# Windowed attention with a mixing layer: one f32 product for three f16 products in A times V

## The chip, the cores and the metric

The kernel runs on one core of a Trainium2 chip. The metric is device microseconds of one execution; of several runs the median is given.

## The reference

The input is q, k and v of 8 batches, 8 heads, 576 positions and 64 values each, in f32, and four weight matrices. Per head there is a causal attention with a window of 128 positions and a linear bias by distance; the heads' outputs, side by side, are x (576 x 512 per batch), which then goes through a mixing layer.

```python
scores = scale * np.matmul(q, k.transpose(0, 1, 3, 2))
mask = (rel >= 0) & (rel < window)
scores = np.where(mask, scores + bias[None], -1000000000.0)
scores = scores - np.max(scores, axis=-1, keepdims=True)
attn = np.exp(scores)
attn = attn / (np.sum(attn, axis=-1, keepdims=True) + 1e-09)
attn_out = np.matmul(attn, v)
# x: heads side by side
theta = x @ w_theta
zr, zi = x * np.cos(theta), x * np.sin(theta)
y = np.einsum('ts,bsd->btd', w_tok_r, zr) + np.einsum('ts,bsd->btd', w_tok_i, zi)
u = x + y
out = u + np.maximum(u @ w_ch, 0.0)
```

## The kernel before

Large products of f32 data are made from f16 parts: a matrix is scaled by a power of two and split into a high part (its f16 rounding) and a low part (the rest in f16), and three products of parts (high x high, high x low, low x high) take the place of one f32 product. q and k are split in the same manner into parts of an f32 format of the tensor engine.

**Heads, pairs, groups.** Heads are worked two at a time (class `Pair`, 32 pairs in all, 4 to a batch), and v is loaded for `GROUP = 4` heads at a time (16 groups, two to a batch; `load_values`, tile `vb`, 128 x 4 x 5 x 65 f32, in a pool `vbp`). The 65th column of v is one, so that the products of the weights with v give the denominator as well.

**One pair.** `Pair.scores` multiplies k and q, `weigh` adds the band and takes the row's extreme on VectorE (DVE, L417) and the exponential on ScalarE (ACT, L420). `Pair.flip` turns the unnormalised weights on the tensor engine (PE, L425), 4 tiles of 128 x 128 to a bank, and brings them to SBUF as `pt`. In batch 0 (`early`) that is one f32 copy on ACT (L428). In batches 1 to 7 ACT writes the high f16 part (L432) and DVE the low one (L433). `Head.values` multiplies `pt` with v (L461): 9 tile products to a head, each of which is three f16 products in batches 1 to 7 (27 to a head) and one f32 product in batch 0. `Head.finish` divides by the denominator (L467 to L470) and writes `x_sb`.

**v in f16.** For batches 1 to 7 `split_values` makes `vh` (ACT, L352, with a memset on GpSimd for the ones, L353) and `vl` (DVE, L354) once for each head. The scale of v comes from `measure` (a maximum of |v| for each head of the group, DVE, L252) and `spread_scales`: a transpose on PE (L259), a maximum, and a product with ones (L265) that brings the scales to all partitions (`spread`). It is called once for each group; for the second group of a batch `batch_scale` derives the factors that the mixing layer uses (`factors`).

**The mixing layer.** `turn` transposes x (L493), multiplies it with w_theta (L514), takes sine and cosine (L528 to L536) and makes z (L539), split into `z_hi` and `z_lo`. `mix` makes y from z and the token weights (L575), `channels` the last product (L597) and the output (L601 to L605).

**Order.** Batch 0's attention (`start`) runs beside the loading and splitting of the weight matrices (`unpack`). Then, per batch, `attend` runs the attention of the next batch in steps with `mix` and part of `channels` of this one; when all heads are done, `rotated` runs `turn` of the next batch beside the rest of `channels`. A planner turns this program order, with priority offsets (`MIX`, `CHAN`, `ROTATE`), into the order of each engine's queue; the offsets are constants in the source. DMAs are issued from SP's queue: q and k (`load_pair`), v (`load_values`), the output.

Of the kernel before, what the change touches and what calls it, by code (L numbers as in the profile page):

```python
# [11 lines left out]
F32 = mybir.dt.float32  # L12
# [3 lines left out]
F16 = mybir.dt.float16  # L16
# [10 lines left out]
PEXP = 14.0  # L27
# [11 lines left out]
RINGS = ([("mx", 2 * NT, 4)] + [("den", NT, 6)] + [("whole", 1, 3), ("vs", GROUP, 3), ("scale", GROUP, 4)]  # L39
         + [(name, width, 1) for name, width in (("whole0", 1), ("vs0", 11), ("scale0", 11), ("most0", 11), ("sum", 17),  # L40
# [11 lines left out]
def attn_moe_kernel(ctx: ExitStack, tc: tile.TileContext, qt, kt, vx, wth, wtok, wch, band, out):  # L52
# [6 lines left out]
    vp = ctx.enter_context(tc.tile_pool(name="vp", bufs=2))  # L59
    vbp = ctx.enter_context(tc.tile_pool(name="vbp", bufs=2))  # L60
# [170 lines left out]
    def load_plain(g):  # L231
        b, h = divmod(GROUP * g, H)
        vb = vbp.tile([128, GROUP, NT, 65], F32, name="vb")
        nc.sync.dma_start(out=vb, in_=vx[b, h:h + GROUP].rearrange("h p (c d) -> p h c d", d=65))
        return vb

# [52 lines left out]
    def measure_first(g):  # L289
        nc.vector.tensor_reduce(out=peaks[0][:, GROUP * g:GROUP * g + GROUP], in_=group_v[g][:, :, :, :64],  # L290
                                axis=mybir.AxisListType.XY, op=ALU.max, apply_absolute_value=True)

    FAMILIES = ((0, 1, 0, 2, 8, 2.0 ** 100), (5, 14, 2, 9, 9, 2.0 ** 120), (1, 5, 11, 4, 10, 2.0 ** 120))

    def scales_first():

        peak = peaks[0]
        for at, source in ((8, wide[:, :1]), (9, sums[:, 8:17]), (10, sums[:, 4:8])):
            nc.vector.tensor_reduce(out=peak[:, at:at + 1], in_=source, axis=mybir.AxisListType.X, op=ALU.max)
        nc.vector.tensor_scalar(out=peak[:, :8], in0=peak[:, :8], scalar1=2.0 ** -100, scalar2=None, op0=ALU.max)  # L300
        scale = spread(peak, 11, "0")
# [11 lines left out]
        nc.vector.tensor_tensor(out=scale[:, 10:11], in0=scale[:, 10:11], in1=rowt[:, 1:], op=ALU.mult)  # L313
        inverse(invs, rows)
        inverse(back, scale[:, 8:11])
# [9 lines left out]
        nc.vector.tensor_scalar(out=fac[:, 1:2], in0=scale[:, 8:9], scalar1=MAGIC, scalar2=None, op0=ALU.mult)  # L325
        batch_scale(0, scale[:, :8])
# [13 lines left out]

    def split_values(n):

        if n < H:
            if n % GROUP == 0:
                group_v[n // GROUP] = load_plain(n // GROUP)
            return (group_v[n // GROUP][:, n % GROUP],), None
# [5 lines left out]
        nc.scalar.activation(vh[:, :, :64], v, AF.Copy, scale=vs)  # L352
        nc.gpsimd.memset(vh[:, :, 64:], 1.0)  # L353
        nc.vector.scalar_tensor_tensor(out=vl, in0=v, scalar=vs, in1=vh[:, :, :64], op0=ALU.mult, op1=ALU.subtract)  # L354
        return (vh, vl), vs

# [11 lines left out]
    class Pair:  # L368


        def __init__(self, p):
            self.p = p
            self.terms = parts.pop(p)
            self.early = p < H // 2
# [47 lines left out]
        def flip(self, bank):  # L422
# [3 lines left out]
            if self.early:  # L426
                pt = ptp.tile([128, 512], F32, name="pt")
                nc.scalar.copy(pt, t_ps)  # L428
                parts_of = [pt]
            else:  # L430
                pt = ptp.tile([128, 2, 512], F16, name="pt")
                nc.scalar.activation(pt[:, 0], t_ps, AF.Copy, scale=2.0 ** PEXP)  # L432
                nc.vector.scalar_tensor_tensor(out=pt[:, 1], in0=t_ps, scalar=2.0 ** PEXP, in1=pt[:, 0],  # L433
                                               op0=ALU.mult, op1=ALU.subtract)
                parts_of = [pt[:, a] for a in range(2)]
            for n, (i, e, j) in enumerate(BANKS[bank]):
                for to in ((0, 1) if i == 0 else (e,)):
                    at = 128 * n + (64 * to if i == 0 else 0)
                    self.pt[i, to, j] = [t[:, at:at + 128] for t in parts_of]

    class Head:
        def __init__(self, n, pair):
            self.n, self.pair = n, pair
            self.b, self.h = divmod(n, H)
            self.tiny = 1.0e-9 * (1.0 if pair.early else 2.0 ** PEXP)

        def ready(self):
            self.v, self.vs = split_values(self.n)
# [383 lines left out]
```

## Time and profile before

| | |
|---|---|
| median of 3 runs | 777.27 us (776.39 to 779.42) |
| profiled execution | 778.7 us, span of its instructions 776.9 us |
| PE (matmul) busy | 695.1 us, 89% |
| PEld (weight load) busy | 520.1 us, 67% |
| DVE busy | 615.4 us, 79% |
| ACT busy | 500.9 us, 64% |
| POOL busy | 216.5 us, 28% |

Busy time is the union of an engine's instructions. Matmuls are pipelined and their ends are modelled, so the distance from one product's start to the next one's says more than a product's duration. Idle time of an engine is put down to the instruction that ended it (its releaser). `s_ps`, `t_ps`, `acc` and `mm` are banks of PSUM; `fixed` is a tile that holds many small operands.

### The profile page before, as it was taken

The page shows a single profiled execution, that of the slowest core. Times are in us where ns is not written, and L with a number is a line of the kernel's source. Part 1 is how long each engine was busy: PE and PEld are TensorE (multiplying, and loading weights), DVE is VectorE, ACT ScalarE, POOL GpSimd, SP SyncE. Part 2 cuts the span into 40 slices and gives each one's busy share as a digit, 9 for nine tenths or more (in the row PEclk, how much of TensorE's full clock was granted, in tenths as well). Part 3 has the DMA queues.
Part 4 walks back from the last instruction along what each step waited for, and adds up shares of the span by engine and source line. Part 5 has one row for each costly group of instructions (what it writes and reads, how often), then busy time and mean ns, then how long its engine had stood idle before and what let it go on. Part 6 is the DMA issues. An engine that isn't in the chain of part 4 may idle for free.

```text
span 776.9 us, 16320 instructions
## 1 busy us (share of the span) xinstructions
PE 695.1 (89%) x6236; PEld 520.1 (67%) x6239; DVE 615.4 (79%) x1668; ACT 500.9 (64%) x964; POOL 216.5 (28%) x237
## 2 busy tenths in 40 slices
PE   4698669789898999899989999899989998999997
PEld 2457555478756886578757885688657875787675
DVE  6998876977877986888688986798688877884844
ACT  4786526676478747786577747775678748754620
POOL 3523211400253113611171115311361116201700
PEclk9775558999999999999999999999999999999999
DMA  8353211121202220123003120132012300101001
GB/s 287 122 168 131 88 35 32 31 66 32 89 24 57 87 74 31 54 67 97 32 24 104 33 81 31 48 96 72 31 57 67 97 24 32 40 2 32 24 8 62
DMA packets 32623, 49.89 MB, mean 64 GB/s; under 512 B 5664, under 2 KB 22048, under 8 KB 32544
## 3 DMA queue, kind: packets, MB, share of 16 engines
q1 hardware_dynamic: 32544, 48.84, 20.3%
q8 instruction: 49, 0.80, 0.4%
q14 instruction: 30, 0.25, 0.1%
HBM read 39.39 MB, written 9.44 MB: 63 GB/s over the span
## 4 chain that ended last, share of the span: by engine, by line
PE 49%; DVE 26%; ACT 16%; issue 4%; DMA 4%; POOL 1%; SPq 0%; DVEq 0%; ACTq 0%; POOLq 0%
PE mm L575 20%; PE acc L461 6%; PE t_ps L425 6%; PE s_ps L402 6%; PE mm L597 5%; DVE f L529 4%; DVE g L531 3%; ACT g L535 3%; PE mm L514 3%; ACT s_sb L420 3%; DVE g L539 2%; ACT f L528 2%; DVE ql L335 2%; DVE x_lo L506 1%; DVE s_sb L417 1%
## 5 line engine op out<-in xcount | busy, mean ns | idle before, releaser
L575 PE MATMUL mm<-wtk_hi,z_hi 128*128 128x288 f16 x576 | 164.7, 289 | 12.3 <-DVE f L526 9.1
L575 PE MATMUL mm<-wtk_lo,z_hi 128*128 128x288 f16 x576 | 162.8, 288 | 0.0
L575 PE MATMUL mm<-wtk_hi,z_lo 128*128 128x288 f16 x576 | 161.3, 288 | 0.0
L575 PEld LDWEIGHTS <-z_hi 128*128 128x128 f16 x1152 | 111.2, 98 | 44.8 <-issue 13.8
L420 ACT ACTIVATE s_sb<-s_sb,fixed 128x256 f32<-128x256 f32 (+1 forms) x256 | 103.7, 470 | 25.9 <-DVE fixed L417 25.2
L417 DVE CUSTOM_DVE_ANT_0 s_sb<-s_ps,bands 128x256 f32<-128x256 f32 (+1 forms) x256 | 85.4, 384 | 0.0
L603 POOL TENSOR_TENSOR xtf<-r,xtf 128x288 f32<-128x288 f32 x56 | 56.0, 1000 | 104.9 <-DVE r L601 104.9
L425 PE MATMUL t_ps<-fixed,s_sb 128*128 128x128 f32 x448 | 76.5, 289 | 4.6 <-ACT s_sb L420 4.4
L432 ACT ACTIVATE pt<-t_ps 128x512 f16<-128x512 f32 x112 | 63.0, 586 | 24.0 <-PE acc L461 19.4
L338 POOL TENSOR_TENSOR kl<-kr,kh 128x576 fp32r<-128x576 f32 x32 | 47.2, 1475 | 108.1 <-ACT kh L337 80.9
L433 DVE SCALAR_TENSOR_TENSOR pt<-t_ps,pt 128x512 f16<-128x512 f32 x112 | 75.6, 681 | 1.2 <-ACT pt L432 0.8
L583 ACT ACTIVATE u_hi<-xtf,fixed 128x288 f16<-128x288 f32 x64 | 33.1, 531 | 67.0 <-DVE xtf L580 66.4
L575 PEld LDWEIGHTS <-z_lo 128*128 128x128 f16 x576 | 57.1, 99 | 14.4
L535 ACT ACTIVATE g<-g,fixed 128x512 f32<-128x512 f32 (+1 forms) x40 | 32.6, 814 | 46.9 <-DVE g L531 46.7
L514 PEld LDWEIGHTS <-x_hi 128*128 128x128 f16 x320 | 31.4, 99 | 46.4 <-issue 16.9
L461 PE MATMUL acc<-vh,pt 128*128 128x65 f16 x1008 | 61.3, 194 | 0.0
L425 PEld LDWEIGHTS t_ps<-fixed,s_sb 128*128 128x128 f32 x448 | 52.7, 148 | 12.7 <-ACT s_sb L420 7.7
L353 POOL MEMSET vh<- 128x5 f16 x56 | 6.7, 120 | 194.0 <-PE acc L461 145.0
L461 PEld LDWEIGHTS <-pt 128*128 128x128 f16 x1512 | 57.1, 98 | 4.6 <-DVE pt L433 0.2
L597 PEld LDWEIGHTS <-wch_hi 128*128 128x128 f16 x512 | 49.2, 98 | 14.6 <-issue 1.1
L485 POOL TENSOR_TENSOR z_lo<-g,z_hi 128x512 f16<-128x512 f32 x32 | 39.5, 1235 | 66.4 <-ACT z_hi L484 65.9
L461 PE MATMUL acc<-vl,pt 128*128 128x64 f16 x504 | 55.4, 193 | 0.0
(153 smaller groups left out, 1647.5 us busy)
## 6 DMA issues: line engine op xcount, KB each, us to landing
vb<-in_vx_dram SPq DMA_DIRECT2D x16, 650.0 KB, 4.2
kr<-in_kt_dram SPq DMA_DIRECT2D x32, 288.0 KB, 2.9
out_dram<-xtf SPq DMA_DIRECT2D x64, 144.0 KB, 1.8
qr<-in_qt_dram SPq DMA_DIRECT2D x32, 144.0 KB, 3.0
qr<-in_qt_dram SPq DMA_DIRECT2D x32, 128.0 KB, 2.9
raw<-in_wtok_dram SPq DMA_DIRECT2D x5, 576.0 KB, 4.8
xtf<-in_wtok_dram SPq DMA_DIRECT2D x4, 576.0 KB, 5.1
raw<-in_wth_dram SPq DMA_DIRECT2D x2, 512.0 KB, 5.9
```

The source lines that it names most:

```text
L338: nc.gpsimd.tensor_tensor(out=kl, in0=kr, in1=kh.bitcast(F32), op=ALU.subtract)
L417: nc.vector.tensor_tensor_reduce(out=sb, in0=ps, in1=bias, scale=2.0 ** -(2 * self.p % H + 1), scalar=3.0e38, op0=ALU.add, op1=ALU.min, ac ...
L420: self.exp = nc.scalar.activation(sb, sb, AF.Exp, bias=least, scale=-1.0)
L425: nc.tensor.transpose(t_ps[:, 128 * n:128 * n + 128], self.sc[i, e][:, 128 * j:128 * j + 128], ident)
L432: nc.scalar.activation(pt[:, 0], t_ps, AF.Copy, scale=2.0 ** PEXP)
L433: nc.vector.scalar_tensor_tensor(out=pt[:, 1], in0=t_ps, scalar=2.0 ** PEXP, in1=pt[:, 0], op0=ALU.mult, op1=ALU.subtract)
L461: nc.tensor.matmul(av[:, i, :r.shape[-1]], l, r, start=(n == 0), stop=(n == len(prods) - 1))
L514: nc.tensor.matmul(t_ps, a[:, c * 128:c * 128 + 128], w[:, c, :], start=(k == 0 and c == 0), stop=(k == len(prods) - 1 and c == 3))
L535: nc.scalar.activation(g[:n], g[:n], AF.Sin, bias=halfpi[:n], scale=rad[:n])
L575: nc.tensor.matmul(y_ps[:, :HALF], z[:, c, m * 128:m * 128 + 128], w[:, c, cs], start=(k == 0), stop=(k == 26))
L597: nc.tensor.matmul(o_ps[:, :HALF], w[:, c, e * 128:e * 128 + 128], u[:, c, cs], start=(k == 0), stop=(k == 11))
L603: (nc.gpsimd if b < B - 1 else nc.vector).tensor_tensor(out=xtf[:, e, cs], in0=r, in1=xtf[:, e, cs], op=ALU.add)
```

## The change

v and the weights of the attention are no longer split in batches 1 to 7. `flip` makes one f32 copy, and `values` multiplies f32 `pt` with f32 `vb`, 9 products to a head, as batch 0 did. `split_values`, the calls of `Head.ready`, the tiles `vh` and `vl` and their pool are gone; the pool of `vb` has three buffers instead of two. The maximum of |v| is now one for a group instead of one for each head, and `spread_scales` runs once for each batch (two columns) instead of once for each group (four columns), since only `batch_scale` uses the result.

```diff
-    vp = ctx.enter_context(tc.tile_pool(name="vp", bufs=2))
-    vbp = ctx.enter_context(tc.tile_pool(name="vbp", bufs=2))
+    vbp = ctx.enter_context(tc.tile_pool(name="vbp", bufs=3))
...
     def measure(g):
-        vb = group_v[g]
-        peak = peaks[g % 2]
-        most = peak[:, :GROUP]
-        nc.vector.tensor_reduce(out=most, in_=vb[:, :, :, :64], axis=mybir.AxisListType.XY, op=ALU.max,
+        most = peaks[g // 2 % 2][:, g % 2:g % 2 + 1]
+        nc.vector.tensor_reduce(out=most, in_=group_v[g][:, :, :, :64], axis=mybir.AxisListType.XYZ, op=ALU.max,
                                 apply_absolute_value=True)
         nc.vector.tensor_scalar(out=most, in0=most, scalar1=2.0 ** -100, scalar2=None, op0=ALU.max)
-        group_v[g] = vb, peak
...
-    def spread_scales(g):
-        vb, peak = group_v[g]
-        scale = spread(peak, GROUP, "")
-        group_v[g] = vb, scale
-        if g % 2:
-            c = rings["scale"].at + (g // 2 - 1) % 2 * 2 * GROUP
-            batch_scale(g // 2, fixed[:, c:c + 2 * GROUP])
...
+    def spread_scales(b):
+        batch_scale(b, spread(peaks[b % 2], 2, ""))
...
-    def split_values(n):
...
-        vb, scale = group_v[n // GROUP]
-        k = n % GROUP
-        v, vs = vb[:, k, :, :64], scale[:, k:k + 1]
-        vh = vp.tile([128, 5, 65], F16, name="vh")
-        vl = vp.tile([128, 5, 64], F16, name="vl")
-        nc.scalar.activation(vh[:, :, :64], v, AF.Copy, scale=vs)
-        nc.gpsimd.memset(vh[:, :, 64:], 1.0)
-        nc.vector.scalar_tensor_tensor(out=vl, in0=v, scalar=vs, in1=vh[:, :, :64], op0=ALU.mult, op1=ALU.subtract)
-        return (vh, vl), vs
...
-            if H // 2 <= p < pairs - 2 and p % 2 == 0:
-                load_values(p // 2 + 1)
+            if p % 2 == 0 and (p < H // 2 or p < pairs - 2):
+                load_values(p // 2 if p < H // 2 else p // 2 + 1)
...
-            if self.early:
-                pt = ptp.tile([128, 512], F32, name="pt")
-                nc.scalar.copy(pt, t_ps)
-                parts_of = [pt]
-            else:
-                pt = ptp.tile([128, 2, 512], F16, name="pt")
-                nc.scalar.activation(pt[:, 0], t_ps, AF.Copy, scale=2.0 ** PEXP)
-                nc.vector.scalar_tensor_tensor(out=pt[:, 1], in0=t_ps, scalar=2.0 ** PEXP, in1=pt[:, 0],
-                                               op0=ALU.mult, op1=ALU.subtract)
-                parts_of = [pt[:, a] for a in range(2)]
+            pt = ptp.tile([128, 512], F32, name="pt")
+            nc.scalar.copy(pt, t_ps)
...
             for i in (0, 2, 3, 4, 1) if self.h % 2 == 0 else (0, 1, 2, 3, 4):
-                prods = []
                 for j, c in enumerate(CHUNKS[i]):
-                    for a, part in enumerate(self.pair.pt[i, self.h % 2, j]):
-                        for e, v in enumerate(self.v):
-                            if a + e < len(self.v):
-                                prods.append((part, v[:, c, :65 if e == 0 else 64]))
-                for n, (l, r) in enumerate(prods):
-                    nc.tensor.matmul(av[:, i, :r.shape[-1]], l, r, start=(n == 0), stop=(n == len(prods) - 1))
+                    nc.tensor.matmul(av[:, i, :], self.pair.pt[i, self.h % 2, j], v[:, c, :], start=(j == 0),
+                                     stop=(j == len(CHUNKS[i]) - 1))
...
-            if p % 2 == 0 and p + 2 < pairs:
-                spread_scales(p // 2 + 1)
+            if p % 4 == 0 and p + 2 < pairs:
+                spread_scales(p // 4)
```

More of the change, by code (lines that the diff above doesn't have):

```diff
@@ L26 @@
 HALF = S // 2
-PEXP = 14.0
 VEXP = 14
@@ L38 @@
 GROUP = 4
-RINGS = ([("mx", 2 * NT, 4)] + [("den", NT, 6)] + [("whole", 1, 3), ("vs", GROUP, 3), ("scale", GROUP, 4)]
-         + [(name, width, 1) for name, width in (("whole0", 1), ("vs0", 11), ("scale0", 11), ("most0", 11), ("sum", 17),
+RINGS = ([("mx", 2 * NT, 4)] + [("den", NT, 6)] + [("whole", 1, 3), ("vs", 2, 3), ("scale", 2, 3)]
+         + [(name, width, 1) for name, width in (("whole0", 1), ("vs0", 5), ("scale0", 5), ("sum", 17),
                                                  ("row", 14), ("inv", 14), ("back", 3), ("lim", 15), ("fac", 15),
@@ L229, in load_pair @@
         return qr, kr
[L231 to L235, printed above, removed]
     group_v = {}
@@ L279, in batch_scale @@
         factors[b] = fs, bs
-    def spread_scales(g):
-        vb, peak = group_v[g]
-        scale = spread(peak, GROUP, "")
-        group_v[g] = vb, scale
-        if g % 2:
-            c = rings["scale"].at + (g // 2 - 1) % 2 * 2 * GROUP
-            batch_scale(g // 2, fixed[:, c:c + 2 * GROUP])
[L289 to L293, printed above, removed]
+    def spread_scales(b):
+        batch_scale(b, spread(peaks[b % 2], 2, ""))
+    FAMILIES = ((0, 1, 0, 2, 2, 2.0 ** 100), (5, 14, 2, 9, 3, 2.0 ** 120), (1, 5, 11, 4, 4, 2.0 ** 120))
     def scales_first():
         peak = peaks[0]
-        for at, source in ((8, wide[:, :1]), (9, sums[:, 8:17]), (10, sums[:, 4:8])):
+        for at, source in ((2, wide[:, :1]), (3, sums[:, 8:17]), (4, sums[:, 4:8])):
             nc.vector.tensor_reduce(out=peak[:, at:at + 1], in_=source, axis=mybir.AxisListType.X, op=ALU.max)
-        nc.vector.tensor_scalar(out=peak[:, :8], in0=peak[:, :8], scalar1=2.0 ** -100, scalar2=None, op0=ALU.max)
-        scale = spread(peak, 11, "0")
+        scale = spread(peak, 5, "0")
         for k in range(2):
@@ L312, in scales_first @@
         power(rowt[:, 1:], wide[:, 3:], -1)
[L313 removed]
+        nc.vector.tensor_tensor(out=scale[:, 4:5], in0=scale[:, 4:5], in1=rowt[:, 1:], op=ALU.mult)
         inverse(invs, rows)
[L315 removed]
+        inverse(back, scale[:, 2:5])
         for k, (lo, hi, at, n, col, top) in enumerate(FAMILIES):
@@ L324, in scales_first @@
                                     op0=ALU.mult)
-        nc.vector.tensor_scalar(out=fac[:, 1:2], in0=scale[:, 8:9], scalar1=MAGIC, scalar2=None, op0=ALU.mult)
-        batch_scale(0, scale[:, :8])
+        nc.vector.tensor_scalar(out=fac[:, 1:2], in0=scale[:, 2:3], scalar1=MAGIC, scalar2=None, op0=ALU.mult)
+        batch_scale(0, scale[:, :2])
     def split_pair(p, raw):
@@ L465, in finish @@
             den = rings["den"].take()[:, :, None]
-            scaled = {} if self.vs is None else {"op1": ALU.mult}
-            nc.vector.tensor_scalar(out=den, in0=av[:, :, 64:65], scalar1=self.tiny, scalar2=self.vs,
-                                    op0=ALU.add, **scaled)
+            nc.vector.tensor_scalar(out=den, in0=av[:, :, 64:65], scalar1=1.0e-9, scalar2=None, op0=ALU.add)
             nc.vector.reciprocal(out=den, in_=den)
@@ L661, in attend @@
             one.finish(x_sb)
-            if new is not None:
-                new.heads[0].ready()
             pair.flip(3)
@@ L670, in attend @@
             two.finish(x_sb)
-            if p % 2 == 0 and p + 2 < pairs:
-                spread_scales(p // 2 + 1)
+            if p % 4 == 0 and p + 2 < pairs:
+                spread_scales(p // 4)
             prepare(p + DEPTH + 2)
-            if new is not None:
-                new.heads[1].ready()
             step(other, 6)
@@ L692, in start @@
             new = Pair(p) if p < H // 2 else None
-            if new is not None:
-                for head in new.heads:
-                    head.ready()
             if new is not None and p % 2 == 0:
-                measure_first(p // 2)
+                measure(p // 2)
             if p == 3:
@@ L758, in attn_moe_kernel @@
         measure(p // 2)
-        spread_scales(p // 2)
         first.append(Pair(p))
-        for head in first[-1].heads:
-            head.ready()
         for tiles in SCORES:
```

11 lines of the change are left out of this document (2 added, 9 removed).

## The prediction, made before the run

> **What bounds the kernel now.** I read the page first (engine shares, clock, chain), then cut the trace into stretches, then asked what the tensor engine (PE) waits for, and last how far apart its products start. From the page:
>
> ```profile
> PE 695.1 (89%) x6236; PEld 520.1 (67%) x6239; DVE 615.4 (79%) x1668; ACT 500.9 (64%) x964; POOL 216.5 (28%) x237
> ...
> PEclk9775558999999999999999999999999999999999
> ...
> PE 49%; DVE 26%; ACT 16%; issue 4%; DMA 4%; POOL 1%; SPq 0%; DVEq 0%; ACTq 0%; POOLq 0%
> ```
>
> Two engines are near full over the whole span, so shares alone don't decide. The clock is low only in the first fifth or so (batch 0 and the weights' unpacking), then full. From about 213 us on the trace repeats, one period per batch. One period, cut behind the first theta products of `turn` and about where the exponentials behind the sines are done (columns: busy time and count of PE, PEld, DVE, ACT, POOL, then clock and DMA; the period is the sum, 84.8 us):
>
> ```profile
> 298.10:332.00 33.90, 29.06 (x223) 19.42 (x220) 25.19 (x51) 25.96 (x44) 16.84 (x15) 1.00 0.14 44
> 332.00:382.90 50.90, 50.69 (x565) 40.72 (x565) 44.61 (x140) 32.68 (x70) 7.92 (x13) 1.00 0.23 69
> ```
>
> The first stretch (the rotation) is a relay between ACT and DVE with gaps on PE. The second, in which the attention of the next batch runs beside `mix`, has PE filled: 50.69 of 50.90 us. DVE is at 44.61 of 50.90 there, the runner-up. Because ends of products are modelled, I check that with what PE waited for, from 104 us to the end (total us, times, longest):
>
> ```profile
> PE mm L514 <- DVE f L529: 10.1, 7, 1.4
> PE mm L575 <- DVE f L526: 9.1, 6, 1.5
> PE t_ps L425 <- ACT last L420: 9.1, 7, 2.3
> PE t_ps L425 <- ACT s_sb L420: 4.4, 14, 0.4
> PE mm L575 <- DVE fixed L417: 2.7, 1, 2.7
> PE mm L265 <- DVE fixed L263: 2.0, 1, 2.0
> PE s_ps L402 <- DVE ql L335: 1.7, 2, 0.9
> PE mm L493 <- DVE x_sb L470: 1.6, 1, 1.6
> ...
> PE mm L265 <- DVE fixed L311: 0.8, 1, 0.8
> PE s_ps L402 <- DVE fixed L417: 0.7, 2, 0.5
> ...
> PE t_ps L425 <- DVE pt L433: 0.2, 1, 0.2
> ```
>
> The four big rows belong to the rotation: the angles (L526, L529) and the exponentials that follow the sines (L420). None of them is a split of v or of the weights. The split of the weights (L433) holds PE up for 0.2 us in the whole kernel, the split of v (L354) for nothing that is listed. So in the attention stretch time is PE's own work, product after product.
>
> **The change part by part.**
>
> *The products.* Batch 0 already multiplies f32 by f32, so the price stands in the trace. Its group, and one head of it at full clock, between the head's first product and the next instruction's:
>
> ```profile
> L461 PE MATMUL acc<-vb,pt 128*128 128x65 f32 x144 | 27.5, 367 | 12.6 <-DVE fixed L178 7.5 <-DVE x_sb L470 4.5 <-ACT pt L428 0.6
> 50.55 2.22 PE L461 MATMUL acc<-vb,pt 128*128 128x65 f32 x18
> 52.61 0.39 PE L425 MATMUL t_ps<-fixed,s_sb 128*128 128x128 f32 x2
> 50.50:52.70 2.20, 2.20 (x23) 2.15 (x20) 1.30 (x4) 2.20 (x5) 0.29 (x1) 1.00 0.88 356
> ```
>
> The trap is in the count. Batch 0 has 8 heads of 9 products, 72, but the trace has x144: each f32 product is two instructions, so 18 make up one head. (The f32 product of `spread`, L265, is two as well.) One head takes 52.61 - 50.55 = 2.06 us, 0.114 us an instruction, with the clock at 1.00. Now the chain in a steady period, with the f16 head:
>
> ```profile
> 362.93 0.11 PE t_ps L425
> 363.04 0.12 PE mm L575
> 363.16 0.11 PE t_ps L425
> 363.27 0.37 PE mm L575 x3
> ...
> 364.47 0.82 PE acc L461 x27
> 365.29 0.47 PE t_ps L425 x4
> ```
>
> 27 f16 products take 0.82 us, 0.030 each. Per head the change costs 2.06 - 0.82 = +1.24 us of PE; 56 heads (batches 1 to 7) make 56 x 1.24 = +69.4 us. It lies on the path, since PE is the bound of the stretch in which all these heads stand, 8 to a batch.
>
> *The scales.* `spread_scales` runs once a batch, not once a group: 14 times become 7. On PE one spread is a transpose and one f32 product, from the chain in the same period:
>
> ```profile
> 350.31 0.11 PE mm L259
> 354.39 0.20 PE mm L265 x2
> ```
>
> 0.31 us each, 7 fewer: -2.2 us. The second of the two spreads at the start (around 112 us) goes too; what it made PE wait (L265 behind L311, 0.8 us) is counted below.
>
> Here is also why a third of the products costs two and a half times as much. In `spread` the product has only GROUP = 4 columns, and each of its two instructions still takes 0.10 us; with 65 columns it is 0.114. So the columns hardly count; what is left is the load of f32 weights, 128 x 128, paid in each instruction. The Trainium skill, "TensorE: Matmul & The Clock Gate", section "Weight-path perf modes", says that the fast weight load isn't given to FP32 weights. The trace agrees in kind: 0.114 us against 0.030.
>
> *What leaves DVE, ACT and POOL.*
>
> ```profile
> L433 DVE SCALAR_TENSOR_TENSOR pt<-t_ps,pt 128x512 f16<-128x512 f32 x112 | 75.6, 681 | 1.2 <-ACT pt L432 0.8
> L354 DVE SCALAR_TENSOR_TENSOR vl<-vb,fixed,vh 128x320 f16<-128x320 f32 x56 | 31.3, 560 | 2.9 <-ACT vh L352 2.5
> L352 ACT ACTIVATE vh<-vb,fixed 128x320 f16<-128x320 f32 x56 | 30.9, 554 | 6.5 <-PE acc L461 6.5
> ```
>
> DVE loses 75.6 + 31.3 = 106.9 us and half of the spreads' small steps, ACT 30.9 us, POOL its memsets. A copy of the transposed weights to f32 stays on ACT. I cost these at a small gain: they lie beside PE's work, as the waits show. The gain's upper bound is every wait above that names something which less DVE work could shorten: 2.7 + 2.0 + 1.7 + 1.6 + 0.8 + 0.7 + 0.2 = 9.7 us, most of it in batch 1, where DVE is fullest. The lower bound is nothing, or below it if the planner orders things worse. I take -5, about half: the waits at 195 to 210 us sit behind DVE's queue and should go, while the one at L263 is the first spread's own chain and stays. Taken away entirely, this cover would matter only if DVE came back as the bound; it will be some 15 us a batch below what it is.
>
> *Waits and queues.* The products now wait for ACT's copy alone, not for ACT and then DVE, so the weights are ready earlier. v's tile is released by the head's last product, not by the split; that is later, and there are three buffers for it instead of two, so the load that SP issues for the next group waits for a group two back. What stands behind that load in SP's queue (q, k, the output) is not held longer, and I cost it at nothing. `measure` keeps its reduction at the same size. The accumulator bank is one as before: the second head's products still wait for the first head's `finish`, under transposes and `mix` products.
>
> *Sum.* +69.4 - 2.2 - 5 = +62.2 us. The profiled execution took 778.7 us, so it becomes 840.9; the median of the runs is 777.27, 1.4 below, and gives 839.5. I say 840, +8%.
>
> **The rivals.**
>
> *The products cost one load, or hide it.* If a f32 product cost one interval of 0.114 us, a head would take 9 x 0.114 = 1.03 us, +0.21 x 56 = +11.8, and the kernel 777.3 + 11.8 - 7.2 = 782 us. The same would come out if the loads ran half under `mix` products that stand between. For it: PE overlaps loads with products elsewhere. Against it: in the fence above f32 transposes stand singly between `mix` products, and 0.11 and 0.12 us simply add; and a head's products stand in one block. Chance 0.04. A rule of the Trainium skill, "FP8 and Floating Point Precision", section "TensorE Precision Notes", leads to this side: true FP32 is 4 passes through the array. Counted by columns alone, 4 x 65 at the 2.4 GHz of "TensorE: Matmul & The Clock Gate", that gives an estimate of 0.108 us a product and 779 us for the kernel; the head above, 0.229 us a product, speaks against counting so.
>
> *DVE is the bound, and the kernel gets faster.* In the attention stretch PEld is busy 40.72 us, DVE 44.61. Were PE's fullness only an effect of modelled ends, DVE's 15 us a batch would come off the path first. PEld would rise by 8 x (18 x 0.114 - 0.82), 9.9 us, to 50.6, just under today's 50.90; with the 9.7 us of waits gone this ends at 777.3 - 7 x 0.3 - 9.7 = 765 us. It decides only if the steady products have gaps between them that a fuller weight load can use. Against it: 0.82 and 0.47 in the chain follow each other without a gap. The Trainium skill, "Perfetto Trace Analysis", section "Identifying the Most-Contended Engine", speaks for this rival: judge PE by the busy share of weight loads, not of matmuls. By that rule the stretch would be DVE's; the spacing of starts in the chain says PE. Chance 0.03.
>
> *The clock falls.* At half clock a head takes about twice its time, and the page's clock row has fives in batch 0. If one head in four ran so, 14 x 2.06 = +29, 869 us. Against it: the head quoted above ran at 1.00 in the midst of f32 work. Chance 0.04.
>
> *The new order is bad.* The planner sees other costs, and the offsets that place `mix` and the channels stay. One or two more waits like those of the rotation (1.4 us each) in each of 7 batches add 10 to 20 us: 850 to 860. Chance 0.07.
>
> That the change does nothing is not to be had: the path it takes is the one that batch 0 shows.
>
> **How the numbers follow.** The forecast has 0.82, with 777.3 + 69.4 - 2.2 - 9.7 = 835 as its lower end if all reachable waits go. I go 7 us lower, to 828, since in batch 1 up to 157 us PE also waits for the relay, and a few of its heads, at 1.24 us each, may fit into such gaps. The upper end is 777.3 + 69.4 - 2.2 = 844.5 with no wait gained, and 854 if the order gets worse by 1.4 us a batch. Range 828 to 854. A change within 0.5%, about 3.9 us, can't be told from none here; that and the part of the first rival that ends there get 0.02, faster 0.03, slower 0.95.
>
> **What would show it.** In the trace after: x1152 f32 products at L461's place (144 + 56 x 18), 2.0 to 2.1 us from a head's first product to what follows, a period of about 94 us instead of 84.8, the attention stretch some 10 us longer with PE still full, the rotation still about 34 us. DVE should be near 505 us, ACT near 470. I am wrong if heads come out at 1.0 us, if the clock row shows fives after 160 us, or if the attention stretch has gaps on PE that DVE or ACT end.

## The result, and the profile after

| | before | after |
|---|---|---|
| median | 776.92 us (776.39 to 779.42) | 821.93 us (820.80 to 823.75, 4 runs) |
| ratio | | 1.0575 (95% interval 1.0543 to 1.0607) |
| profiled execution | 778.7 us, span 776.9 | 821.12 us, span 819.3 |

The change makes the kernel slower, as forecast, but by 42.4 us of span (45.0 us by the medians) where 62.2 were forecast. The time lies 6 us below the low end of the range. Of the runs below, one execution of `e_dead` (891.6 us) and one of `o_after_m0` (947.6 us) had a much lower granted clock than the others of the same kernel and are left out of the figures. From the page of after: engine shares, clock, chain.

```profile
PE 739.5 (90%) x5714; PEld 572.8 (70%) x5714; DVE 532.3 (65%) x1473; ACT 477.2 (58%) x908; POOL 207.6 (25%) x181
...
PEclk8686579999999999999999999999999999999999
...
PE 50%; DVE 20%; ACT 16%; DMA 4%; issue 3%; POOL 2%; SPq 0%; ACTq 0%; DVEq 0%
...
L403 PE MATMUL acc<-vb,pt 128*128 128x65 f32 x1152 | 149.0, 282 | 13.5 <-DVE fixed L176 8.1
...
L386 ACT COPY pt<-t_ps 128x512 f32<-128x512 f32 x128 | 72.5, 583 | 102.2 <-PE t_ps L384 101.9
```

DVE lost 83 us and PE gained 44. The count of f32 products is 1152, as worked out, and the clock row has no five behind batch 0. One period after, cut as the one before was (columns: busy time and count of PE, PEld, DVE, ACT, POOL, then clock and DMA):

```profile
303.36:337.26 33.90, 29.63 (x211) 20.50 (x209) 24.93 (x49) 26.01 (x44) 16.72 (x14) 1.00 0.14 42
337.26:395.33 58.07, 57.44 (x499) 48.13 (x499) 33.74 (x114) 29.52 (x62) 6.62 (x6) 1.00 0.21 61
```

The rotation is what it was, 33.9 us. The attention stretch grew from 50.9 to 58.1 us, not by the 10 us forecast, and PE still fills it. What PE waited for, from 104 us to the end:

```profile
PE mm L455 <- DVE f L470: 8.7, 6, 1.5
PE mm L516 <- DVE f L467: 7.6, 5, 1.5
PE t_ps L384 <- ACT last L379: 7.0, 7, 1.1
PE t_ps L384 <- ACT pt L386: 2.8, 6, 0.5
PE mm L455 <- ACT xtf L448: 2.5, 3, 1.5
PE mm L252 <- DVE fixed L250: 1.7, 2, 1.3
```

These are the rotation's rows again, but for the fourth: behind the rotation, once a batch, a flip waits up to 0.5 us for ACT's f32 copy, which is new. The waits for DVE's small steps before a mixing product (2.7 us before) and for `ql` (1.7) are gone or down to half a microsecond.

**Where the 42.4 us lie.** I cut both traces at the first angle instruction on ACT of each batch's `turn` (L528 before, L469 after). Stage lengths in us:

| | to the first `turn` | batch 1 | batches 2 to 6 | batch 7 | end |
|---|---|---|---|---|---|
| before | 124.58 | 89.06 | 84.51, 84.78, 84.44, 84.55, 84.41 | 76.54 | 64.06 |
| after | 121.64 | 90.44 | 91.32, 91.97, 92.38, 91.92, 91.91 | 83.74 | 64.02 |
| difference | -2.94 | +1.38 | +6.8 to +7.9 | +7.20 | -0.04 |

Cut like this, the stages of batches 2 to 6 hold eight heads each, that of batch 7 seven, and nine of the 56 changed heads lie ahead of batch 2. Batches 2 to 7 give 44.0 us, where the parts gave 56.7 (47 heads and five spreads fewer). All before them gives -1.6, where the parts gave +5.5 (nine heads, two spreads fewer and the 5 us of waits). So 12.7 of the missing 19.8 us are in the repeating stretch and 7.1 ahead of it.

For the repeating stretch I sum, over one period, the distance from each product's start to the next one's, put down to the first product's kind, less what PE waited. The last column counts the changes between the score products, which use 64 of the array's 128 rows, and all other products; it matters below. Means of batches 2 to 6, all at a clock of 1.00:

| us per period | A·V | mix | channels | theta | flips | scores | rest | PE waits | period | changes |
|---|---|---|---|---|---|---|---|---|---|---|
| before | 6.74 | 27.42 | 12.22 | 12.08 | 8.02 | 8.45 | 4.83 | 4.77 | 84.5 | 28 |
| after | 15.48 | 27.00 | 12.02 | 12.12 | 7.91 | 8.13 | 4.48 | 4.75 | 91.9 | 24 |

A·V grew by 8.74 us, not 9.92. Everything else on PE became 1.4 us shorter, of which 0.33 is the second spread (in "rest"). PE's waits did not change in sum.

### The profile page after: what moved, and what is told of

Its sections match the earlier page's. It is cut to its first block, busy times and chain, and to the rows that moved or that the text cites. A ratio compares the mean times of both kernels' runs of the same rounds, so it can differ in the third digit from the quotient of the medians.

```text
span 819.3 us, 14881 instructions
## 1 busy us (share of the span) xinstructions
PE 739.5 (90%) x5714; PEld 572.8 (70%) x5714; DVE 532.3 (65%) x1473; ACT 477.2 (58%) x908; POOL 207.6 (25%) x181
## 4 chain that ended last, share of the span: by engine, by line
PE 50%; DVE 20%; ACT 16%; DMA 4%; issue 3%; POOL 2%; SPq 0%; ACTq 0%; DVEq 0%
PE mm L516 18%; PE acc L403 12%; PE t_ps L384 5%; PE mm L538 5%; PE s_ps L361 5%; PE mm L455 4%; ACT s_sb L379 3%; ACT g L476 3%; DVE g L472 3%; DVE f L470 3%; DVE ql L312 2%; POOL z_lo L426 2%; DVE g L480 2%; DMA vb<-in_vx_dram 2%; ACT f L469 1%
## 5 line engine op out<-in xcount | busy, mean ns | idle before, releaser
L403 PE MATMUL acc<-vb,pt 128*128 128x65 f32 x1152 | 149.0, 282 | 13.5 <-DVE fixed L176 8.1
L516 PE MATMUL mm<-wtk_lo,z_hi 128*128 128x288 f16 x576 | 160.8, 286 | 0.0
L403 PEld LDWEIGHTS acc<-vb,pt 128*128 128x128 f32 x1152 | 145.5, 202 | 17.2 <-issue 10.9
L516 PEld LDWEIGHTS <-z_hi 128*128 128x128 f16 x1152 | 109.2, 98 | 40.8 <-issue 10.6
L386 ACT COPY pt<-t_ps 128x512 f32<-128x512 f32 x128 | 72.5, 583 | 102.2 <-PE t_ps L384 101.9
L544 POOL TENSOR_TENSOR xtf<-r,xtf 128x288 f32<-128x288 f32 x56 | 53.9, 963 | 192.4 <-DVE r L542 192.4
L384 PE MATMUL t_ps<-fixed,s_sb 128*128 128x128 f32 x448 | 72.2, 282 | 3.8 <-ACT pt L386 3.1
L521 DVE SCALAR_TENSOR_TENSOR xtf<-mm,fixed,xtf 128x288 f32<-128x288 f32 x64 | 32.0, 513 | 37.3 <-PE mm L516 37.3
L361 PE MATMUL s_ps<-kh,qh 64*128 64x256 f32 (+1 forms) x256 | 46.6, 343 | 7.7 <-DVE fixed L376 7.2
L455 PE MATMUL mm<-wth_hi,x_hi 128*128 128x512 f16 x160 | 41.8, 384 | 11.9 <-DVE f L470 8.7
```

The lines of the kernel that those rows point to most:

```text
L361: nc.tensor.matmul(ps[:, e, off:off + kn], qm[rows, q0:q0 + qn], km[rows, k0:k0 + kn], start=(j == 0), stop=(j == last))
L384: nc.tensor.transpose(t_ps[:, 128 * n:128 * n + 128], self.sc[i, e][:, 128 * j:128 * j + 128], ident)
L403: nc.tensor.matmul(av[:, i, :], self.pair.pt[i, self.h % 2, j], v[:, c, :], start=(j == 0), stop=(j == len(CHUNKS[i]) - 1))
L455: nc.tensor.matmul(t_ps, a[:, c * 128:c * 128 + 128], w[:, c, :], start=(k == 0 and c == 0), stop=(k == len(prods) - 1 and c == 3))
L516: nc.tensor.matmul(y_ps[:, :HALF], z[:, c, m * 128:m * 128 + 128], w[:, c, cs], start=(k == 0), stop=(k == 26))
L544: (nc.gpsimd if b < B - 1 else nc.vector).tensor_tensor(out=xtf[:, e, cs], in0=r, in1=xtf[:, e, cs], op=ALU.add)
```

## The experiments

My theory after the result: PE is the bound; a f32 product costs two instructions, and each one pays a load of 128 x 128 weights; what DVE and ACT lose is worth nothing in the repeating stretch; the rest of the difference is the order of PE's queue, which the planner makes anew for each kernel. The rivals: the products are paid by columns, or DVE's relief is what made up for the missing part.

**1. Every f32 product twice** (`e_twice`).

```diff
-                for j, c in enumerate(CHUNKS[i]):
+                for j, c in enumerate(CHUNKS[i] * 2):
+                    j = j % len(CHUNKS[i])
```

> The changed kernel, with every f32 product of the weights and v issued twice (the second set starts the sum anew, so the result is the same): 36 instructions a head instead of 18. Theory (PE is the bound of the attention stretch, and a f32 instruction costs 0.112 us there, one load of f32 weights): a head grows by 18 x 0.112 = 2.0 us, a batch in the steady part by 16 us, from 91.9 to about 108; the kernel from 822 to 925 to 945 us (48 heads of batches 2 to 7 make +96, batch 1 up to +16, batch 0 some). Rival (part of a head's products lies in gaps of PE, and the 20 us that the prediction was too high were hidden there): the period grows by 12 us or less, the kernel ends under 905 us.

Measured 977.78 us (one run, beside before at 778.41), above the 925 to 945 expected. One head of it in the timeline of PE (start, length, instruction):

```profile
385.16 4.13 PE L404 MATMUL acc<-vb,pt 128*128 128x65 f32 x36
389.12 0.82 PE L384 MATMUL t_ps<-fixed,s_sb 128*128 128x128 f32 x6
```

36 instructions take 389.12 - 385.16 = 3.96 us, 0.110 each, in one block. A·V of a period went from 15.48 to 31.6 us, the +16.1 expected. But the period went to 113.9, +22.0. The other 5.9 us are not A·V: scores 8.1 to 12.5, `mix` 27.0 to 29.0, and 62 changes in place of 24. Nothing was added to these products; only their neighbours in PE's queue changed. This miss led to experiments 7 and 9.

**2. 100 columns for 65** (`e_wide`). Each product of A·V reads 35 columns more; the rest is as in after.

```diff
-                    nc.tensor.matmul(av[:, i, :], self.pair.pt[i, self.h % 2, j], v[:, c, :], start=(j == 0),
+                    at = 65 * (NT * (self.n % GROUP) + c)
+                    nc.tensor.matmul(av[:, i, :], self.pair.pt[i, self.h % 2, j], v[:, at:at + 100], start=(j == 0),
```

> The changed kernel, with 100 columns of v in each product instead of 65 (the 35 more are the next chunk's and land in columns of the bank that nobody reads). Theory (a f32 instruction costs its load of weights, not its columns): start to start stays 0.112 us, the kernel 822 us, within 3. Rival (four passes of the columns in each instruction, which would give 65 columns the same 0.11 us): start to start becomes 0.112 x 100 / 65 = 0.172 us, 18 x 0.06 = +1.08 us a head, the period 91.9 + 8.6 = 100.5 us, the kernel about 880 us.

Measured 823.57 us (one run), against 821.93 for after. In the timeline of PE:

```profile
380.84 0.81 PE L406 MATMUL acc<-vb,pt 128*128 128x100 f32 x6
381.49 0.29 PE L519 MATMUL mm<-wtk_hi,z_hi 128*128 128x288 f16 x1
```

Six instructions in 0.65 us, 0.108 each, with half as many columns again. So the columns don't set the price of these products. That their load of weights does is what is left, and it is not shown by itself: no run here changed the number of weights in a load.

**3. Reduced f32** (`e_f32r`): `pt` and a copy of v (66 columns, ACT) in the rounded f32 format that q and k use. 9 instructions a head, of the same size, with less precision in A·V.

```diff
-            pt = ptp.tile([128, 512], F32, name="pt")
+            pt = ptp.tile([128, 512], F32R, name="pt")
...
+        round_v[g] = vbp.tile([128, GROUP, NT, 66], F32R, name="vr")
+        nc.scalar.copy(round_v[g][:, :, :, :65], vb)
```

> The changed kernel, with weights and v rounded to the tensor engine's reduced f32 format (ACT writes the weights in it, and copies v once a group): one instruction a product, 9 a head, at a lower precision. Theory (each instruction pays one load of weights): 9 x 0.112 = 1.0 us a head instead of 1.95, -0.95 x 8 = -7.6 us a batch, the period 91.9 - 7.6 = 84.3 us, the kernel 822 - 53 = 769 us (762 to 775), so a little under the kernel before. Rival (columns set the price): 9 instructions of 66 columns in one pass come near the f16 product's 0.03 us, 0.3 us a head, the period about 78.7 us, the kernel about 730 us.

Measured 799.06 us (796.99 to 799.65), ratio to before 1.0264 (1.0243 to 1.0284), above the 762 to 775 us expected. One period, batch 6, has a clock of 1.00 throughout and lasts 86.2 us. In it A·V takes 8.39 us, 1.05 a head: half of after's, as two instructions against one demand. The scores take 9.54 us for 8.13, with 38 changes. The other periods lasted 87.8 to 91.1. Three windows around the end of a rotation show why (the granted clock is the third figure from the end):

```profile
233.30:243.50 10.20, 7.83 (x59) 5.14 (x57) 10.09 (x21) 6.78 (x14) 3.65 (x3) 1.00 0.26 73
243.50:253.70 10.20, 9.63 (x49) 7.79 (x49) 6.10 (x23) 8.38 (x18) 1.41 (x1) 0.50 0.04 6
253.70:263.90 10.20, 10.20 (x94) 8.77 (x92) 4.35 (x19) 5.76 (x14) 0.00 (x0) 1.00 0.21 57
```

Behind the relay, with PE busy 7.83 of 10.20 us, the clock fell to 0.50 for 10.2 us and cost about 4 us of that period. Neither before nor after has such a dip in batches 2 to 7.

**4 to 6. The splits put back, unused** (`e_dead` both, `e_deadw` the weights' low part on DVE alone, `e_deadv` the split of v alone). The work runs as in before on DVE and ACT, and nothing reads its output.

```diff
+    def split_dead(n):
+        v = group_v[n // GROUP][:, n % GROUP, :, :64]
+        nc.scalar.activation(deadh, v, AF.Copy, scale=ones)
+        nc.vector.scalar_tensor_tensor(out=deadl, in0=v, scalar=ones, in1=deadh, op0=ALU.mult, op1=ALU.subtract)
...
+            if self.p >= H // 2:
+                nc.vector.scalar_tensor_tensor(out=dead, in0=t_ps, scalar=2.0 ** 14, in1=pt,
+                                               op0=ALU.mult, op1=ALU.subtract)
...
+                split_dead(new.heads[0].n)
```

> The changed kernel, with the removed work on DVE and ACT put back without use: per bank the low part of the weights on DVE, per head a high part of v on ACT and a low part on DVE, into scratch tiles; the products stay f32. Theory (what the prediction missed is on PE: a head is 1.95 us instead of 2.06, and the changes between kinds of products got cheaper; only the start and batch 1 gained from the emptier DVE): the steady period stays 91.9 us within 0.5, start and batch 1 together lose 3 to 8 us, the kernel 825 to 830 us. Rival (the emptier DVE is what gave the 20 us): the period goes to 94 us, the kernel to 836 to 842 us.

> The changed kernel with only the low part of the weights put back on DVE, unused (16 instructions of 0.68 us a batch). The run with all splits put back came out at about 840 us, and its profile, taken at a clock of 0.85, shows PE waiting for DVE for only 0.4 us in a period: 100.0 us of PE's own products, 85 us at full clock, and hardly a gap. Theory A (DVE is not in the way; if the time grows, the clock fell or PE's order got dearer): at full clock the steady period is 91.9 us within 1, the kernel 822 to 828 us, and whatever lies above that shows as fives in the clock row. Theory B (DVE is in the way after all, 2 us a batch for all splits): PE waits for DVE in the attention stretch, the period is 93 us or more at full clock, the kernel 832 to 836 us.

> The changed kernel with only the split of v put back, unused (a head: 0.55 us on ACT, 0.55 us on DVE). Theory A: period 91.9 us within 1, the kernel 822 to 827 us, any more is the clock. Theory B: period 92.5 us or more at full clock with PE waiting for DVE or ACT, the kernel 826 to 832 us.

Measured: `e_dead` 839.1 to 851.4 us in three runs, ratio to before 1.0848 (1.0771 to 1.0926). `e_deadw` 831.05 (829.86 to 832.24), `e_deadv` 833.39 (833.21 to 833.58). So work that nobody reads costs 9, 11 and 19 us by the medians, more than the theory allowed in all three. That looks like the rival: DVE matters. For the repeating stretch the period of `e_deadw` says otherwise. First its two stretches, then what PE waits for in it:

```profile
306.53:340.43 33.90, 29.69 (x213) 20.53 (x211) 24.88 (x49) 25.98 (x44) 16.73 (x14) 1.00 0.13 41
340.43:399.70 59.27, 59.10 (x499) 48.78 (x499) 42.20 (x130) 29.32 (x63) 6.63 (x6) 1.00 0.20 60
```

```profile
PE mm L527 <- DVE f L478: 1.5, 1, 1.5
PE mm L466 <- DVE f L481: 1.4, 1, 1.4
PE t_ps L392 <- ACT last L387: 1.1, 1, 1.1
PE mm L549 <- DVE xtf L532: 0.2, 1, 0.2
```

DVE has 8.5 us more in the attention stretch than in after (42.20 against 33.74), and PE waits for it less, not more: 59.10 of 59.27 us busy. The period is 93.17 us, +1.25. The additions are PE's own: scores 9.30 for 8.13, A·V 15.79 for 15.48, and 36 changes for 24. In `e_deadv` a period at a clock of 1.00 is 91.7, that of after. Of the 12.1 us of its trace over after's, 10.1 stand ahead of batch 2: 127.06 us to the first `turn` (+5.4) and 95.12 in batch 1 (+4.7). Most of the other 2 stand in two periods with 3.4 us at half clock. Where the loss of `e_dead` stands isn't known, since no trace shows it at full clock.

**7. The second spread put back, unused** (`e_spread`).

```diff
+            if p % 4 == 2 and p + 2 < pairs:
+                spread(peaks[(p + 2) // 4 % 2], 2, "")
```

> The changed kernel with the second spread of each batch put back, unused (transpose, small f32 product, four small DVE steps; 7 times). Theory (PE pays 0.31 us each, and the start, where the second spread stood in PE's queue, 1 to 3 us): 822 + 2.2 + 1 to 3 = 825 to 827 us. Rival (it lies beside other work): 822 us within 1.

Measured 852.75 us (845.27 to 856.86), ratio 1.0947 (1.0880 to 1.1013), where 825 to 827 were expected: some 30 us over after (24 in the profiled execution), for about 0.3 us of PE work a batch. A period at a clock of 1.00 is 95.96 us. The spread itself takes 0.26 of the +4.0; scores take 10.37 for 8.13 and `channels` 13.22 for 12.02, with 44 changes.

**8. Fewer f16 products** (`m_hi`): before, with the weights' low part left out, so 18 products a head and no low-part work on DVE, with weights of 11 bits.

```diff
-                pt = ptp.tile([128, 2, 512], F16, name="pt")
-                nc.scalar.activation(pt[:, 0], t_ps, AF.Copy, scale=2.0 ** PEXP)
-                nc.vector.scalar_tensor_tensor(out=pt[:, 1], in0=t_ps, scalar=2.0 ** PEXP, in1=pt[:, 0],
-                                               op0=ALU.mult, op1=ALU.subtract)
-                parts_of = [pt[:, a] for a in range(2)]
+                pt = ptp.tile([128, 512], F16, name="pth")
+                nc.scalar.activation(pt, t_ps, AF.Copy, scale=2.0 ** PEXP)
+                parts_of = [pt]
```

> The kernel before, without the low part of the weights in batches 1 to 7 (the weights keep 11 bits, in numerator and denominator alike; v keeps both parts): 18 f16 products a head instead of 27, and no weight split on DVE. The run with the reduced f32 format asked for this. Theory (PE is the bound, a f16 product costs 0.030 us): -9 x 0.030 x 56 = -15 us, and 1 to 4 us more in batch 1 from the emptier DVE: 758 to 763 us, steady period 82.4 us, if the clock holds. Rival (less work on PE makes it idle enough after the rotation for the clock to fall, as it did for 10 us in four periods with the reduced f32 format): fives in the clock row after 160 us, 5 us lost for each, 765 to 785 us.

Measured 773.24 us (768.20 to 776.44), ratio 0.9934 (0.9896 to 0.9971), where 758 to 763 were expected. A·V fell by 2.1 us a period, to 4.64, as expected. Scores rose by 0.9 and `mix` by 0.4, with 36 changes for 28, and one period had 6.8 us at half clock. Most of the gain was taken back on PE, with DVE 61 of 84 us busy.

**9. The same work in another order** (`o_after_m50`, `o_after_m0`, `o_dead_m0`, `m_hi_m0`). Only the offset that places `mix` against the attention is changed, in after, in `e_dead` and in `m_hi`. Counted in PE's queue as built, over the whole kernel, after has 202 changes; with MIX at -50 there are 374, with MIX at 0 there are 200 in both after and `e_dead` (284 at -100), and 178 in `m_hi` (260 at -100).

```diff
-MIX, MIX0, CHAN, CHAN0, ROTATE = -100, 0, -60, -300, 100
+MIX, MIX0, CHAN, CHAN0, ROTATE = -50, 0, -60, -300, 100
```

> The changed kernel with MIX = -50: the same work on all engines, but 374 changes between half-array and whole-array products in PE's queue instead of 202. Theory A: +172 x 0.11 = +19 us, 841 us (836 to 848), and PE waits for DVE no more than before. Theory B (the count of changes is only a companion of something else): 822 us within 5.

> Control for the run beside it: the changed kernel with MIX = 0, 200 changes in PE's queue against 202. Theory A: 822 us within 3. If MIX = 0 is better or worse for another reason, it shows here.

> All splits put back unused on DVE and ACT, as in the run that took about 840 us, and one number of the order changed: the offset MIX is 0 instead of -100. In PE's queue as built, the changes between half-array products (the scores) and whole-array products then number 200 instead of 284; the changed kernel has 202. In the profiles so far such a change costs 0.11 us over the usual spacing. Theory A (order on PE, not DVE's load, made that run slow): 84 fewer changes, -9 us, and the steady period comes to 92 us; with the start and batch 1 still 3 to 8 us longer the kernel takes 825 to 832 us. Theory B (DVE's load did it): the work on DVE is the same, so 836 to 842 us.

> The kernel before without the low part of the weights (18 f16 products a head; the weights keep 11 bits), with MIX = 0: 178 changes in PE's queue instead of the 260 of the run that took 773 us. Theory A: -82 x 0.11 = -9 us, 764 us (760 to 768). Rival: an emptier PE lets the clock fall in more periods, 770 us or more with fives in the clock row.

`o_after_m50`: 856.63 us (854.72 to 858.54), where 836 to 848 were expected. Not one instruction is added, the clock of batches 2 to 6 stays at 1.00, PE waits 5.0 us a period (4.75 in after), and the period is 98.5 us, +6.6. The direction is confirmed; the price is 6.6 / 34 = 0.19 us for a change, not the 0.11 I had taken. The rows show how it comes about. After, a stretch of PE's timeline, and then one of `o_after_m50`:

```profile
381.83 0.28 PE L361 MATMUL s_ps<-kh,ql 64*128 64x256 f32 x2
381.95 0.28 PE L361 MATMUL s_ps<-kl,qh 64*128 64x256 f32 x2
...
382.30 0.28 PE L361 MATMUL s_ps<-kl,qh 64*128 64x256 f32 x2
382.51 0.30 PE L516 MATMUL mm<-wtk_hi,z_hi 128*128 128x288 f16 x1
```

```profile
470.19 0.33 PE L361 MATMUL s_ps<-kh,qh 64*128 64x256 f32 x2
470.36 0.28 PE L361 MATMUL s_ps<-kh,ql 64*128 64x256 f32 x1
470.57 0.42 PE L516 MATMUL mm<-wtk_hi,z_hi 128*128 128x288 f16 x2
...
471.02 0.27 PE L347 MATMUL mm<-kl,qh 128*128 128x192 f32 x1
471.23 0.38 PE L361 MATMUL s_ps<-kh,ql 64*128 64x256 f32 x1
471.54 0.42 PE L516 MATMUL mm<-wtk_lo,z_hi 128*128 128x288 f16 x2
471.89 0.38 PE L361 MATMUL s_ps<-kl,qh 64*128 64x256 f32 x1
472.20 0.30 PE L516 MATMUL mm<-wtk_hi,z_lo 128*128 128x288 f16 x1
```

Score products come in pairs (the two heads of a pair, each on its half of the rows). Inside a run of pairs one pair takes 0.12 us, 381.83 to 381.95. The pair ahead of a `mix` product takes 0.21, 382.30 to 382.51: leaving the half-array products costs 0.09. In the second fence the planner put `mix` and others between the two products of one pair. Then a single product takes 0.31 us (471.23 to 471.54, 471.89 to 472.20), for half the work. So a change costs 0.1 us by itself, and more where it breaks a pair.

`o_after_m0` has as few changes in a period as after, 24, but 842.17 us (841.57 to 849.33 in three runs), ratio 1.0832 (1.0782 to 1.0882). Its clock falls behind every rotation, 10.2 us at half clock in most periods, which last about 95 us. The page's clock row:

```profile
PEclk9685589999989999799989999799988999799999
```

`o_dead_m0` is the same: 24 changes, 10.2 to 13.7 us at half clock in most periods, 864.41 us (860.08 to 869.96). Both were expected near 822 to 832; the expectation knew the changes and not the clock. `m_hi_m0` came out at the expected number, 765.29 us (763.15 to 766.93), ratio 0.9814 (0.9787 to 0.9842), in part by luck: it has 20 changes a period, but also 3.4 to 6.8 us at half clock in every period, which the forecast left to the rival. Its batches 4 to 7 are no shorter than those of `m_hi`, and the gain stands ahead of them and at the end. It is 1.9% faster than before, at the price of the weights' low part.

**10. What sets the time ahead of batch 2?** (`e_deadv2`): the split of v put back unused from batch 2's heads on, meant to add nothing up to the end of batch 1.

```diff
-            if new is not None:
+            if new is not None and new.heads[0].n >= 2 * H:
                 split_dead(new.heads[0].n)
```

(against `e_deadv`, which also has the first heads' splits.)

> The changed kernel with the split of v put back, unused, for the heads of batches 2 to 7 only. Theory (the split hurts where DVE and ACT set the pace, in the start and in batch 1, and nowhere else): 121.6 and 90.4 us for these two parts as in the changed kernel, steady periods of 91.7 to 92 us, the kernel 822 us within 3. Rival (the split hurts everywhere, or reorders the whole program): 828 us or more.

Measured 834.39 us (834.07 to 834.72), as slow as `e_deadv`. That is not the test it was meant to be. The splits need only v, and the planner put them far ahead of their place in the program: four run at 111 to 117 us, ahead of the first `turn`, and eight in batch 1, at 183 to 188 and 211 to 216 us. (In `e_deadv` eight run by 95 us, and four at 114 to 120.) Batch 1 of it, and then of after:

```profile
125.26:224.07 98.81, 88.36 (x662) 66.94 (x663) 60.94 (x174) 59.51 (x114) 18.36 (x15) 0.93 0.15 43
```

```profile
121.64:212.08 90.44, 84.01 (x667) 64.97 (x668) 55.11 (x166) 55.11 (x106) 18.02 (x15) 0.98 0.16 47
```

The eight splits in batch 1 stand in the counts of DVE (x174 for x166) and ACT (x114 for x106). Batch 1 is 8.4 us longer, with PE idle for 10.4 us in place of 6.4 and 13.7 us at half clock in place of 3.4, and the stretch ahead of it is 3.6 us longer. Comparing the starts of the same products in both traces shows where the 12 us come from. The products of A·V at 102 us start 0.3 us earlier than in after. Behind the first four splits they start 2.6 us later, and the first `turn` 3.6. The splits at 183 to 188 us add nothing. Behind those at 211 to 216 us it is 3 us more, where PE waits 2.7 us for DVE; after waits 1.1 us for the same step. Two of the splits, and that wait:

```profile
116.69 0.54 DVE L237 SCALAR_TENSOR_TENSOR deadl<-vb,fixed,deadh 128x320 f16<-128x320 f32 x1
215.96 0.55 DVE L237 SCALAR_TENSOR_TENSOR deadl<-vb,fixed,deadh 128x320 f16<-128x320 f32 x1
217.64 1.12 PE L546 MATMUL mm<-u_hi,wch_hi 128*128 128x288 f16 x4 [2.70 <-DVE r L550]
```

The 5 us in between arise around 155 us, where no split runs and the clock is at half for 6.8 us. So the theory isn't refuted: 6 to 7 of the 12 us stand right behind split work on DVE and ACT ahead of batch 2, and the other 5 stay open. The rest follows the repeating part: 91.75 us a period at a clock of 1.00.

**11. The f32 way where PE waits anyway** (`m_half1`): before, with f32 products in the first four heads of batch 1 alone, and the first group's spread done later. Full precision.

```diff
-            self.early = p < H // 2
+            self.early = p < H // 2 + 2
...
+            if p == H // 2:
+                spread_scales(p // 2)
...
-        spread_scales(p // 2)
```

> The kernel before, with the f32 way (no splits, 9 f32 products a head) also in the first four heads of batch 1, a third buffer for v, and the first spread of batch 1 moved behind these heads; all else as before, at full precision. Theory: the start 3 us shorter, batch 1 4 x 1.08 = 4.3 us longer in products and up to 5 us shorter without the splits at its head; the steady periods stay 84.5 us (220 changes in PE's queue against 222): 772 to 776 us against 777 to 778. Rival (the start's gain comes from the single spread, not from the splits): 778 to 782 us.

Measured 775.99 us (773.78 to 778.10, 12 runs) against 777.96 (17 runs), ratio 0.9969 (0.9954 to 0.9984): faster by 0.3%, less than what one would act on. The stretch to the first `turn` became 119.93 us, 4.7 less than in before, and batch 1 92.12, 3.1 more, with 13.7 us at half clock where the profiled execution of before had 6.8.

## Why the prediction was wrong

**Right: the bound.** PE bounds the repeating stretch and the added work lies on the path. Shown by experiment 1 and by `e_deadw`, where 8.5 us more of DVE left PE without a gap. The rival with DVE as the bound is refuted for the repeating stretch, in both directions; ahead of batch 2 experiment 10 speaks for it. The Trainium skill, "Perfetto Trace Analysis", section "Identifying the Most-Contended Engine", judges PE by its share of the peak rate and by the busy share of weight loads. Here the share of weight loads was below DVE's before the change, 40.72 against 44.61 us, and yet PE was the bound; so in this case the spacing of starts decided and not that share.

**Right: two instructions to a product.** The count of 1152 and experiment 3, where one instruction in place of two halves A·V, show it. "The products cost one load" is refuted.

**Wrong size: a head.** The term was 2.06 - 0.82 = +1.24 us. Measured over the periods it is 15.48 / 8 - 6.74 / 8 = 1.935 - 0.843 = +1.09. The quoted f32 head of batch 0 followed score products, so its first interval held a change that I didn't know of: 0.16 us to the second instruction, against 0.06 in heads that follow other products. After, one head lies between `mix` products like this:

```profile
377.63 1.23 PE L403 MATMUL acc<-vb,pt 128*128 128x65 f32 x10
378.69 0.29 PE L516 MATMUL mm<-wtk_hi,z_lo 128*128 128x288 f16 x1
...
379.06 0.33 PE L403 MATMUL acc<-vb,pt 128*128 128x65 f32 x2
379.23 0.29 PE L516 MATMUL mm<-wtk_hi,z_lo 128*128 128x288 f16 x1
...
380.45 0.78 PE L403 MATMUL acc<-vb,pt 128*128 128x65 f32 x6
381.07 0.60 PE L384 MATMUL t_ps<-fixed,s_sb 128*128 128x128 f32 x4
```

1.06 + 0.17 + 0.62 = 1.85 us for its 18 instructions. The error is 0.15 x 47 = 7 us in batches 2 to 7. One head, from a place that isn't typical, was taken for 56. The Trainium skill, "TensorE: Matmul & The Clock Gate", section "LDWEIGHTS (loading the stationary operand)", gives columns / 1.2 ns for a weight load, 107 ns for 128; 18 of them are an estimate of 1.92 us a head. The trace agrees with it (1.935), and it would have been the better term.

**Missing: the neighbours.** The sum held all other products at their old spacing, without a reason. They became about 1.0 us a period shorter, some 5.5 us in batches 2 to 7. In the table that is `mix` -0.42, scores -0.32, `channels` -0.20 (half of it four products that fell ahead of a cut) and flips -0.12. Sorting the distances of batches 3 to 6 by which product follows which says more. There are 14 entries into a run of score products a period before and 12 after. An entry costs 0.09 us over the usual distance, and so does leaving, so the four fewer changes are worth about 0.4 us. The other 0.6 us lie in flips that no score product follows: 61 of 0.121 us before, 56 of 0.111 after. Six of them stood right behind f16 products of A·V and took 0.140 us, where those behind f32 products take 0.115; two stood ahead of a wait for ACT's exponential and count 0.27, and after has no such wait. That order alone can move a period is shown: `o_after_m50` has the instructions of after and a period 6.6 us longer. The rival "the new order is bad" had the right resource and the wrong form: it looked for waits, while the price of an order stands between products that never wait. Here its sign was luck. One more unused spread turned it by +4 us a period.

**Wrong size: the part ahead of batch 2.** Forecast +5.5, measured -1.6. The waits I had put at -5 did go in part: PE's idle time in batch 1 fell from 9.75 to 6.40 us. But the clock was at half for 3.4 us there in place of 6.8, and the stretch up to the first `turn`, for which the sum had hardly anything, became 2.9 us shorter, with one f32 head more in it. Three traces point at the splits of v there. Four of them put back at 111 to 117 us moved the first `turn` by 3.6 us (experiment 10), the twelve of `e_deadv` by 5.4, and before without its two at 117 us, and with a later spread, came to it 4.7 us earlier (experiment 11). A spread put back didn't delay it: 120.81 us in `e_spread`, 121.64 in after. So the relief of DVE and ACT was most likely worth more here than the listed waits. How much of the rest is order and clock is not settled: these are single traces, executions of before alone spread over 5 us, and no run held the clock still while the order changed.

**Right: the small terms.** The spread gave 0.33 us a batch (0.31 forecast). PE's waits in the repeating stretch stayed at 4.8 us. DVE ended at 532 us and not near 505, which cost nothing: its group rows add up to 81 us in a period of before, of which the busy time is 69.8, since neighbouring instructions overlap. Taking out some 15 us of rows took 11.1 us from the busy time. The third buffer of v started nothing that PE waits for in the period; ACT's copy costs one wait of 0.5 us. "The clock falls" didn't come true for after, but it did, at 3.4 to 13.7 us a time, for several of its relatives, so its chance of 0.04 was too small for a kernel whose PE rests in every rotation.

In sum: 7 us by a head that wasn't typical, 5.5 us by the neighbours, 7 us ahead of batch 2. The range failed because its lower end was built from waits alone: the price of a head stood in it as exact, and the closer spacing of the other products was not among its cases.

## What to carry to other kernels

When an engine is full, price its instructions by start-to-start distances averaged over a whole period, and look at what stands ahead of the sample: a first interval can hold a switch that belongs to the neighbour. Here a full-precision f32 product took two instructions of 0.11 us, with 65 columns as with 100, and three f16 products took 0.09 us together, so the split parts were the cheaper way. In a kernel whose queues a planner orders, any edit is also a change of order: count the changes between half-array and whole-array products in the old and the new queue, and rerun one experiment with another order before believing in a difference of a few per cent. Look in the trace where the planner put the work of an edit, too: in experiment 10 it was not where the program has it.

## What the runs showed of the hardware

- An f32 product's instruction took 0.103 to 0.112 us whether it had 65 or 100 columns (experiment 2), and a reduced-f32 product took one such interval (1.05 us for 9).
- Going between products on 64 rows and products on 128 rows cost about 0.1 us a change, and 0.3 us instead of 0.06 for a single score product whose pair was broken (experiment 9).
- The granted clock fell to 0.50 for 3.4 to 13.7 us at a time, mostly behind a rotation, although PE was busy 77% of the 10 us ahead of it (experiment 3). In `e_spread` it fell for 3.4 us at 394 and at 684 us, behind 10.2 us in which PE was busy throughout. The Trainium skill, "TensorE: Matmul & The Clock Gate", section "What's actually happening", ties the half clock to a window of about 3.4 us of idle time. The dips come in multiples of 3.4 us, which agrees; no fully idle window stands ahead of them, which doesn't.
